# Reordering the opening of a retention-and-bilinear-FFN kernel: states and outputs in the order 0, 2, 1, 3, v scalings off VectorE, the last output in the scores' banks

## The chip, the cores and the metric

One core of one Trainium2 chip. The metric is the device time of one execution, in microseconds. Before the change it is 334.72 us (median of 4 runs, 334.57 to 334.90).

All runs named below computed the right result.

Every experiment was timed beside runs of the kernel before on the same chip in the same job. Where "over before" or "under before" is said of an experiment, it is the difference of these two medians. A ratio with an interval is the mean time of one kernel's fast runs over that of the other's of the same rounds, so it isn't quite the ratio of the medians quoted.

Names: PE is the matmul engine, PSUM the memory that it writes its results to. In the profiles DVE is VectorE, ACT is ScalarE, POOL is PoolE and SP is SyncE. The *span* of an execution runs from its first to its last instruction, and the *granted clock* is the share of PE's full clock that the profile records, so 0.5 is half clock.

## The reference, cut to what matters

```python
# q, k, v: [8 batches, 8 heads, 576 positions, 64]
scores = (1/sqrt(64)) * q @ k.T
ret    = scores * D            # D[i,j] = gamma_h ** (i-j) for i >= j, else 0
x      = (ret @ v) as [4608 tokens, 512]
out    = ((x @ w_a) * (x @ w_b)) @ w_out      # d_ff = 1536
```

The kernel splits gamma ** (i-j) into a factor on the query side (the tables `qs`, applied when an output leaves PSUM) and a factor on v (`vs`, the "v scaling"), with a triangular mask on the scores. Positions are taken in chunks, and what earlier chunks contribute is carried in a state matrix.

## The kernel before

The feed-forward part is by far the larger. It can start only when the first 512 tokens of x exist and when the first of three pieces of w_a has arrived (384 of its 1536 columns). The *opening* makes these tokens in four steps, each 256 tokens of four of the eight heads: steps 0 and 1 are the first four heads, steps 2 and 3 the others. Step 1 needs the state left by step 0; step 3 that of step 2. The order of the steps differs by kind of work: before computes scores in the order 0, 2, 1, 3, but states and outputs in the order 0, 1, 2, 3.

Each step needs loads of q, k, v (256 KB each, issued by SyncE), casts to bf16, transposes on PE with a copy out of PSUM, scores on PE with a mask on VectorE, v scaled by `vs`, a state, and an output whose scaling on VectorE writes x. `warm(n, 256)` issues n filler matmuls, meant to keep PE's clock up.

```python
    STEPS = [(0, 0), (1, 0), (0, 1), (1, 1)]
    for i, which in ((0, Q), (0, K), (2, K), (2, Q), (1, Q), (0, V),
                     (1, K), (1, V), (3, K), (3, Q), (2, V), (3, V)):
        load_step(*STEPS[i], which)                 # SyncE's queue

    def load_w(f0, f1, which="ab"):                 # weights, PoolE's queue, fp32 -> bf16
        if "a" in which:
            nc.gpsimd.dma_start(wa_sb[:, :, f0:f1], wa_r[:, :, f0:f1])
        ...
    def values_step(i, kp, on):                     # half of a step's v scaling
        n, hh = STEPS[i]
        on.tensor_tensor(...)                       # 128x256
    ...
    cast_step(2, K, "pool")                         # the opening, cut to PoolE's part
    ...
    cast_step(2, Q, "pool")
    ...
    values_step(0, 0, pool_)                        # waits for v of step 0
    values_step(0, 1, vector)
    ...
    load_w(0, W1, "a")                              # first piece of w_a
    values_step(1, 0, vector)
    ...
    state_step(3, (0,))
    for F in range(3):
        ffn_begin(F)                                # six matmuls on x of steps 0 and 1
    output_step(3)
    warm(3, 256)
```

In the traces PoolE runs its instructions in the order in which they are written. So `load_w(0, W1, "a")` is issued when PoolE is through with all PoolE work written above it (9.84 us, right behind the scaling that starts at 9.28, below). Later, two 128-row tiles (items 4 and 5) are cast with `cast(i, "dve")`: q on ScalarE, k on VectorE, v on PoolE.

## Time and profile before

| | before |
|---|---|
| median time | 334.72 us |
| span of the profiled execution | 332.6 us |
| PE busy | 324.5 us, 98% |
| seventh feed-forward matmul starts | 20.04 us |

From the profile page: part 1 (busy us and share of the span of each engine), the granted PE clock in 40 slices of the span (tenths), and the engines' shares of the chain that ended last.

```profile
PE 324.5 (98%) x3616; PEld 167.5 (50%) x3616; DVE 166.0 (50%) x305; ACT 128.2 (39%) x270; POOL 113.8 (34%) x146
...
PEclk9999999999999999999999999999999999999999
...
PE 94%; ACT 2%; DVE 2%; issue 1%; ACTq 0%; DVEq 0%
```

PE is the bound almost everywhere. The opening is different: PE does small pieces and fillers there, and what counts is the time from which the feed-forward matmuls run unbroken. I measure this by the start of the **seventh** feed-forward matmul: six can run before the last output, the seventh needs everything. From then on the program is PE-bound, so a shift of the seventh should shift the end. This is the end of the opening in the timeline of PE (start us, duration us, engine, line, operation, output and inputs, count, and in brackets the idle time before it and what ended it):

```profile
17.20 1.47 PE L754 MATMUL pa<-xT,wa_sb 128*128 128x512 bf16 x6
18.51 0.39 PE L395 MATMUL o<-qkT,state_after 128*128 128x128 bf16 x4
18.83 0.42 PE L404 MATMUL o<-sT,vb 64*64 64x128 bf16 x16
19.18 0.50 PE L836 MATMUL w<-ones 128*128 128x256 bf16 x3
20.04 0.81 PE L772 MATMUL pa<-xT,wa_sb 128*128 128x512 bf16 x3 [0.36 <-DVE xT L411]
```

L754 are the first six, L772 begins with the seventh. In between lie the last output step, three fillers, and a wait of 0.36 us for VectorE's scaling.

These are PoolE's instructions from the timeline of before between 7 and 11 us.

```profile
7.38 0.61 POOL L315 CAST qkb<-qf 128x512 bf16<-128x512 f32 x1 [0.23 <-DMA qf<-in_q_dram]
9.28 0.62 POOL L319 TENSOR_TENSOR vb<-vf,vs 128x256 bf16<-128x256 f32 x1 [1.28 <-DMA vf<-in_v_dram]
9.84 0.93 POOL L266 DMA_DIRECT2D wa_sb<-in_moe_w_a_dram  x1
```

PoolE idles 1.28 us until v of step 0 lands, scales it, and only then issues the first weight load, at 9.84 us. And these are the DMA packets of one microsecond, 12 to 13 us, by queue (packets, MB, share of the 16 engines' time, which passes 100% where packets overlap; q1 carries q, k and v, q0 the weights):

```profile
q1 hardware_dynamic: 554, 0.27, 110.9%
q0 software_dynamic: 14, 0.01, 6.9%
```

In this microsecond the weights have hardly begun (their first packet comes at 12.6 us), and q, k and v have the DMA engines almost to themselves.

### The profile page before, as it was taken

How to read it: one execution, taken by the hardware profiler on the slowest of the kernel's cores; microseconds unless marked ns; L12 is line 12 of the kernel's file. 1: busy time of each engine (PE TensorE's matmuls, PEld its weight loads, DVE VectorE, ACT ScalarE, POOL GpSimd, SP SyncE). 2: the span in 40 equal slices, each digit the busy share in tenths (PEclk: the TensorE clock that was granted, in tenths of full speed). 3: DMA queues.
4: the chain of work that ended last, by engine and by line, in shares of the span. 5: the costliest groups of instructions: out<-in, count | busy, mean ns of one | idle time of the engine just before them, and what ended most of it. 6: DMA issues, size and time to landing. Idle time of an engine off the chain costs nothing.

```text
span 332.6 us, 8646 instructions
## 1 busy us (share of the span) xinstructions
PE 324.5 (98%) x3616; PEld 167.5 (50%) x3616; DVE 166.0 (50%) x305; ACT 128.2 (39%) x270; POOL 113.8 (34%) x146
## 2 busy tenths in 40 slices
PE   6999999999999999999999999999999999999996
PEld 3744446858644554545454545454545454444443
DVE  5845446456745464566247623762476347414321
ACT  7734833434515344353134323523352334213321
POOL 4780038570548468157044503470340000000000
PEclk9999999999999999999999999999999999999999
DMA  7999999999999999897599259955960420020002
GB/s 207 254 183 208 198 224 209 233 190 183 168 207 236 220 213 257 175 220 132 131 227 213 51 140 191 203 90 142 198 105 3 131 62 0 3 95 32 2 32 95
DMA packets 146151, 50.37 MB, mean 151 GB/s; under 512 B 130624, under 2 KB 141632, under 8 KB 146112
## 3 DMA queue, kind: packets, MB, share of 16 engines
q1 hardware_dynamic: 141360, 45.10, 65.0%
q0 software_dynamic: 4752, 4.72, 8.7%
q8 instruction: 28, 0.46, 0.6%
q14 instruction: 11, 0.09, 0.1%
HBM read 37.75 MB, written 9.44 MB: 142 GB/s over the span
## 4 chain that ended last, share of the span: by engine, by line
PE 94%; ACT 2%; DVE 2%; issue 1%; ACTq 0%; DVEq 0%
PE pa L772 28%; PE pb L787 28%; PE po L807 28%; PE o L692 2%; PE o L705 1%; PE sc L666 1%; PE kv L615 1%; ACT qs L224 1%; PE kv L371 1%; PE w L836 1%; PE tp L328 0%; PE o L404 0%; PE pa L754 0%; PE sc L343 0%; ACT qkT L330 0%
## 5 line engine op out<-in xcount | busy, mean ns | idle before, releaser
L792 DVE TENSOR_TENSOR hT<-ha,pb 128x512 bf16<-128x512 bf16 (+1 forms) x120 | 75.9, 634 | 97.8 <-PE pb L787 85.4
L780 ACT CAST ha<-pa 128x512 bf16<-128x512 f32 (+1 forms) x120 | 64.8, 543 | 123.1 <-PE pa L772 122.4
L787 PE MATMUL pb<-xT,wb_sb 128*128 128x512 bf16 (+1 forms) x480 | 111.8, 358 | 0.1
L772 PE MATMUL pa<-xT,wa_sb 128*128 128x512 bf16 (+1 forms) x474 | 110.3, 358 | 1.1 <-DVE xT L532 0.6
L807 PE MATMUL po<-wo_sb,hT 128*128 128x512 bf16 (+1 forms) x444 | 97.3, 374 | 0.0
L787 PEld LDWEIGHTS <-wb_sb 128*128 128x128 bf16 x480 | 46.7, 98 | 47.3 <-issue 1.1
L772 PEld LDWEIGHTS <-wa_sb 128*128 128x128 bf16 x474 | 45.3, 98 | 46.9 <-issue 2.5
L807 PEld LDWEIGHTS <-hT 128*128 128x128 bf16 x444 | 42.4, 98 | 47.0
L555 POOL CAST qkb<-qf 64x1024 bf16<-64x1024 f32 x15 | 15.5, 1030 | 86.9 <-DMA qf<-in_q_dram 82.7
L818 DVE COPY osb<-po 128x512 f32<-128x512 f32 (+1 forms) x18 | 12.2, 676 | 44.8 <-PE po L807 44.8
L560 POOL TENSOR_TENSOR vb<-vf,vs 128x1024 bf16<-128x1024 f32 x15 | 28.5, 1902 | 8.3 <-DMA vf<-in_v_dram 4.5
L816 ACT COPY osb<-po 128x512 f32<-128x512 f32 (+1 forms) x19 | 10.9, 575 | 45.3 <-PE po L807 45.3
L714 DVE TENSOR_TENSOR xT<-o,qs 128x512 bf16<-128x512 f32 x30 | 19.6, 681 | 5.5 <-PE o L705 5.5
L634 DVE TENSOR_TENSOR sums<-kv,sums 128x256 f32<-128x256 f32 x47 | 19.9, 422 | 4.6 <-PE kv L615 3.1
L675 DVE TENSOR_TENSOR sT<-sc,mask 128x512 bf16<-128x512 f32 x30 | 19.8, 680 | 0.0
L559 POOL CAST qkb<-qf 64x512 bf16<-64x512 f32 x30 | 17.8, 619 | 1.8 <-DMA qf<-in_q_dram 1.2
L559 POOL CAST qkb<-kf 64x512 bf16<-64x512 f32 x30 | 17.6, 614 | 0.9
L646 ACT CAST states<-sums 64x512 bf16<-64x512 f32 (+1 forms) x30 | 17.2, 574 | 0.5
L555 POOL CAST qkb<-kf 64x1024 bf16<-64x1024 f32 x15 | 15.5, 1035 | 5.4 <-DMA kf<-in_k_dram 4.9
L836 PE MATMUL w<-ones 128*128 128x256 bf16 (+1 forms) x40 | 8.5, 342 | 1.5 <-DVE ones L202 1.5
L431 POOL TENSOR_TENSOR vb<-vf,vs 128x512 bf16<-128x512 f32 x2 | 2.1, 1060 | 21.7 <-DMA vf<-in_v_dram 21.7
L224 ACT ACTIVATE qs<-qs,biasq,lgp 128x384 f32<-128x384 f32 (+1 forms) x12 | 8.0, 733 | 2.4 <-DVE qs L247 2.4
(103 smaller groups left out, 158.3 us busy)
## 6 DMA issues: line engine op xcount, KB each, us to landing
qf<-in_q_dram SPq DMA_DIRECT2D x32, 256.0 KB, 4.6
kf<-in_k_dram SPq DMA_DIRECT2D x32, 256.0 KB, 5.2
vf<-in_v_dram SPq DMA_DIRECT2D x32, 256.0 KB, 5.0
out_dram<-osb SPq DMA_DIRECT2D x31, 256.0 KB, 2.2
wo_sb<-in_moe_w_out_dram POOLq DMA_DIRECT2D x3, 512.0 KB, 17.0
out_dram<-osb SPq DMA_DIRECT2D x10, 128.0 KB, 2.8
qf<-in_q_dram SPq DMA_DIRECT2D x8, 128.0 KB, 4.1
kf<-in_k_dram SPq DMA_DIRECT2D x8, 128.0 KB, 5.4
```

What stands on the lines that cost most here:

```text
L555: nc.gpsimd.tensor_copy(qkb[0:64, w], t[0:64])
L559: nc.gpsimd.tensor_copy(to[:, :, 1 - r], fro[:, :, r])
L560: nc.gpsimd.tensor_tensor(vb.rearrange("p (k h d) -> p k h d", k=2, h=H), vf.rearrange("p (k h d) -> p k h d", k=2, h=H), vs2[:, n % BL].u ...
L634: nc.vector.tensor_tensor(sums[:, i], own, prev, op=ALU.add)
L646: nc.scalar.copy(into[half(1 - r)].rearrange("p (k a) c d -> p a k (c d)", a=2)[:, 1, which.start // 2: which.stop // 2], sums[half(r)].re ...
L675: nc.vector.tensor_tensor(sT[:, on].rearrange("p c k s -> p (c k) s"), sc[:, on].rearrange("p c k s -> p (c k) s"), mask3.unsqueeze(1).to_ ...
L714: nc.vector.tensor_tensor(x_of(t0, 128).rearrange("p c (a s) -> p c a s", a=2), o[:, :, :, kp].rearrange("p a c s -> p c a s"), qs[:, :, s ...
L772: nc.tensor.matmul(pa[:, 0:n], wa_sb[:, c, fs], xT[:, c], start=(c == 0), stop=(c == NC - 1))
L780: nc.scalar.copy(ha[:, 0:n], pa[:, 0:n])
L787: nc.tensor.matmul(pb[:, 0:n], wb_sb[:, c, fs], xT[:, c], start=(c == 0), stop=(c == NC - 1))
L792: nc.vector.tensor_tensor(hT[:, F, 0:n], has[F][:, 0:n], pb[:, 0:n], op=ALU.mult)
L807: nc.tensor.matmul(po[:, 0:width], hT[:, F, u * 128:(u + 1) * 128], wo_sb[:, F, cols], start=(F == 0), stop=(F == NF - 1))
```

## The change

Its intent: get the opening's critical engines out of each other's way. The state and the output of step 2 come before those of step 1, because step 1 depends on step 0 and step 2 doesn't; the scores ran 0, 2, 1, 3 already. VectorE, busy for 13.4 of the first 20 us, keeps the work that reads PSUM and gives its v scalings after step 0 to PoolE and ScalarE. The `qs` tables are spread out instead of being made in one block. The last output goes to the PSUM banks of the scores, so it needn't wait for the scaling of the output before it.

```diff
-    for i, which in ((0, Q), (0, K), (2, K), (2, Q), (1, Q), (0, V),
-                     (1, K), (1, V), (3, K), (3, Q), (2, V), (3, V)):
+    for i, which in ((0, Q), (0, K), (0, V), (2, Q), (2, K), (1, K),
+                     (1, Q), (2, V), (3, K), (3, Q), (1, V), (3, V)):
 ... (clearing of two_states: from VectorE's start to PoolE, after the opening)
+        if on is nc.scalar:
+            for h in range(4):
+                on.mul(to[:, h], fro[:, h], by[:, h:h + 1])
 ...
-    def output_step(i):
+    def output_step(i, place=None):
 ...
+            o = place.tile([128, 2, 512], FP32, tag="sc", name="o0")
 ... (the opening's order, cut)
-    cast_step(2, K, "pool")
-    cast_step(2, Q, "pool")
-    values_step(0, 0, pool_)
-    values_step(0, 1, vector)
+    values_step(0, 0, nc.scalar)
+    values_step(0, 1, vector)
+    cast_step(2, Q, "pool")
+    cast_step(2, K, "pool")
     load_w(0, W1, "a")
 ...
+    for kp in (0, 1):
+        values_step(1, kp, pool_)
+    values_step(3, 0, nc.scalar)
+    values_step(3, 1, pool_)
+    load_w(W1, W2)
+    score_step(3)
+    state_step(1, (0,))
+    state_step(3, (0,))
+    output_step(1)
+    output_step(3, ps_sc)
     for F in range(3):
         ffn_begin(F)
-    output_step(3)
-    warm(3, 256)
```

More of the change, by code (lines that the diff above doesn't have):

```diff
@@ L191, in make_masks @@
     def make_masks():
+        nc.gpsimd.memset(two_states, 0.0)
         nc.gpsimd.iota(idxv_i, pattern=[[256, BL], [128, 2]], base=0,
@@ L202 @@
     nc.vector.memset(ones, 1.0)
+    idxp_f = const.tile([128, 6], FP32)
+    nc.vector.tensor_copy(idxp_f, idxp_i)
+    nc.vector.tensor_scalar_add(idxp_f[64:128, 4:5], idxp_f[64:128, 4:5],
+                                -float(S))
     lgp = const.tile([128, HP], FP32)
@@ L208 @@
     nc.vector.memset(biasq, math.log(scale))
-    idxp_f = const.tile([128, 6], FP32)
-    nc.vector.tensor_copy(idxp_f, idxp_i)
-    nc.vector.tensor_scalar_add(idxp_f[64:128, 4:5], idxp_f[64:128, 4:5],
-                                -float(S))
     vs = const.tile([128, H, 6], FP32)
@@ L260 @@
     state_after = const.tile([128, 2, 2, HP, 128], BF16)
-    for t in (state_after, two_states):
-        nc.vector.memset(t, 0.0)
+    nc.vector.memset(state_after, 0.0)
     def load_w(f0, f1, which="ab"):
@@ L318, in values_step @@
         n, hh = STEPS[i]
-        on.tensor_tensor(
-            by_parity(natural[n, hh][1])[:, :, kp], given(i, 2)[:, :, kp],
-            vs[:, 4 * hh:4 * hh + 4, 2 * n + kp].unsqueeze(2)
-            .to_broadcast([128, 4, D]), op=ALU.mult)
+        to, fro = by_parity(natural[n, hh][1])[:, :, kp], given(i, 2)[:, :, kp]
+        by = vs[:, 4 * hh:4 * hh + 4, 2 * n + kp]
+        if on is nc.scalar:
+            for h in range(4):
+                on.mul(to[:, h], fro[:, h], by[:, h:h + 1])
+        else:
+            on.tensor_tensor(to, fro, by.unsqueeze(2)
+                             .to_broadcast([128, 4, D]), op=ALU.mult)
     def transpose_step(i, w, on):
@@ L387, in output_step @@
         sT = scored.pop((n, hh))
-        o = ps_o[0].tile([128, 2, 512], FP32, tag="o", name="o0")
+        if place is None:
+            o = ps_o[0].tile([128, 2, 512], FP32, tag="o", name="o0")
+        else:
+            o = place.tile([128, 2, 512], FP32, tag="sc", name="o0")
         for a in (0, 1):
@@ L841 @@
     warm(8, 512)
-    for c in range(HP):
-        make_qs(c, 0, 512)
+    make_qs(0, 0, 512)
     for i in range(4):
@@ L847 @@
     cast_step(0, K, "dve")
-    transpose_step(0, Q, "dve")
-    cast_step(2, K, "pool")
-    transpose_step(0, K, "act")
+    make_qs(1, 0, 512)
+    transpose_step(0, Q, "act")
+    transpose_step(0, K, "dve")
+    values_step(0, 0, nc.scalar)
+    values_step(0, 1, vector)
+    make_qs(2, 0, 512)
+    cast_step(2, Q, "pool")
     warm(4, 256)
     score_step(0)
-    transpose_step(2, K, "act")
+    warm(3, 256)
+    state_step(0, (0, 1))
+    warm(1, 256)
+    transpose_step(2, Q, "dve")
+    cast_step(2, K, "pool")
+    cast_step(1, K, "act")
     warm(4, 256)
+    transpose_step(2, K, "dve")
+    warm(4, 256)
+    load_w(0, W1, "a")
     cast_step(1, Q, "act")
-    cast_step(2, Q, "pool")
-    transpose_step(2, Q, "act")
-    warm(4, 256)
-    transpose_step(1, Q, "dve")
-    values_step(0, 0, pool_)
-    values_step(0, 1, vector)
-    warm(2, 256)
     score_step(2)
-    cast_step(1, K, "act")
-    state_step(0, (0, 1))
-    warm(4, 256)
     transpose_step(1, K, "act")
-    load_w(0, W1, "a")
-    values_step(1, 0, vector)
-    warm(3, 256)
     output_step(0)
-    values_step(1, 1, pool_)
+    transpose_step(1, Q, "act")
+    values_step(2, 1, pool_)
+    values_step(2, 0, pool_)
+    make_qs(3, 0, 512)
     load_w(0, W1, "b")
+    warm(5, 256)
     score_step(1)
-    cast_step(3, K, "act")
-    state_step(1, (0,))
-    transpose_step(3, K, "act")
-    cast_step(3, Q, "pool")
+    warm(1, 256)
+    cast_step(3, Q, "act")
+    state_step(2, (0, 1))
+    cast_step(3, K, "pool")
     warm(4, 256)
     transpose_step(3, Q, "act")
-    values_step(2, 0, vector)
-    values_step(2, 1, pool_)
-    output_step(1)
-    state_step(2, (0, 1))
-    score_step(3)
-    values_step(3, 1, pool_)
-    warm(4, 256)
-    output_step(2)
-    values_step(3, 0, pool_)
-    load_w(W1, W2)
-    state_step(3, (0,))
+    transpose_step(3, K, "dve")
+    output_step(2)
+    for kp in (0, 1):
[6 more added lines that the diff above has]
+    state_step(3, (0,))
+    output_step(1)
+    output_step(3, ps_sc)
     for F in range(3):
         ffn_begin(F)
-    output_step(3)
-    warm(3, 256)
     load_w(W2, DFF)
```

## The prediction

> **What bounds the kernel now.** PE. The busy table gives PE 324.5 of 332.6 us; the chain of waits is 94% PE, and after 20.04 us the timeline shows only a few PE gaps (0.55 us at 55.2, 0.36 at 71.5, 0.33 at 92.6). The first 20 us differ: the PE work there is small pieces and 40 filler matmuls, and what matters is when the feed-forward matmuls can run without a break. In the timeline the first six (0.216 us apart) run from 17.2 us, then the last output step (18.51 to 19.2), three fillers and the last scaled x (VectorE, 19.30 to 19.99) come between, and the seventh starts at 20.04. I call this "FFN-7 = 20.04".
>
> **Limits inside the opening.** Twelve 256 KB loads land about 0.9 us apart, from 3.8 to 14.5 us (issue-to-landing marks). VectorE is the crowded engine: four masks of 1.22 us (start 7.70, 10.21, 13.15, 15.71), four scalings of 0.69, casts, copies, v scalings of 0.42 to 0.58. ScalarE does four qs tables in one block (3.58 to 6.63), so the second transpose copy waits until 6.54 and the scores start only at 7.16.
>
> **What the change does.**
> 1. Two qs tables (0.76 each) leave ScalarE's path to the first transposes; one VectorE memset (0.48) leaves the path to the first cast (4.85). Estimate: first scores at 6.1 to 6.3, first mask at 6.9 (it has a v scaling before it), 0.8 us earlier.
> 2. This lead is not kept: the second mask needs the loads and casts of step 2's q and k, and stays near 10.2.
> 3. VectorE loses three v scalings and its Q copies for later steps; PoolE and ScalarE take them. Four ScalarE multiplications of 128x64 replace one 128x256 operation. The Trainium skill ("ScalarE: Activation LUTs", What ACT_TABLE_LOAD costs) gives 280 ns + 0.833 N with a pointer operand, overlapping by 93: about 1.0 us for four. This trace has eight 128x18 activations in 0.98 us, 0.105 apart, so I estimate 0.6 to 1.0. Both are off VectorE.
> 4. Third and fourth masks: about 12.5 and 15.5 instead of 13.15 and 15.71.
> 5. The last two outputs no longer share the output banks, so their matmuls needn't wait for the scaling between; but the last one waits for the last mask to leave the score banks, and for the last state copies (v of steps 1 and 3 land last, 13.6 and 14.5; PoolE scales 0.62 each). The six first matmuls now come after both outputs and cover the last scaling.
>    Estimate: output 1 done at 16.6, output 3 at 17.3, x of step 1 at 17.5, FFN begins at 17.6 and runs on: FFN-7 at about 18.9 to 19.1.
>
> **Critical part.** About 1.0 us of FFN-7; filler matmuls and the order of loads cost nothing by themselves. Behind it the weights must keep up: the second pieces land 22.5 and 25.0 and are used at 24.9 and 28.3, the third at 28.1 and 31.3, used at 31.8 and about 35, w_out 33.9 to 39.4, used from 40.4. About 2.4 us of slack everywhere, so a 1 us shift fits. The rest of the program should shift as a block.
>
> **Predicted:** 333.7 us, range 333.0 to 334.5. Faster by over 2%: 0.01; within 2%: 0.98; slower by over 2%: 0.01.
>
> **What would show it.** First scores PE near 6.2; second mask near 10.2; last scaling ending before 18.5; seventh FFN matmul near 19.0, no gap before it; same PE gaps afterwards.
>
> **What would make it wrong.** The earlier weight load delaying the last v loads; ScalarE's queue, in order, holding a state copy behind a cast that waits for a load; the PoolE scalings of step 1 coming late and delaying the states; W1's second half landing after 20 us; later gaps at 55 us growing since their loads haven't moved.

## The result, and the profile after

The kernel after takes **337.21 us** (median of 4 runs, 336.79 to 337.59) against 334.72 before: ratio 1.0074, 95% interval 1.0056 to 1.0091. Measured again beside before in a later job (r_after): 337.34 against 334.77, ratio 1.0082 (1.0067 to 1.0097). It is 2.5 us slower, where about 1 us faster was predicted.

| | before | after |
|---|---|---|
| span of the profiled execution | 332.6 us | 335.1 us |
| mean granted PE clock | 1.000 | 0.995 |
| masks of the four steps start | 7.70, 10.21, 13.15, 15.71 | 6.68, 10.42, 12.63, 15.48 |
| last v landed | 14.46 us | 17.00 us |
| seventh feed-forward matmul | 20.04 us | 22.56 us |

(The landings are marks in the trace.) The span grew by 2.5 us, and so did the start of the seventh matmul. All of the loss in this profile is therefore in the opening; the PE gaps after it are those of before, shifted (0.55 us at 57.7 against 55.2, 0.36 at 74.0 against 71.5, 0.33 at 95.2 against 92.6). Up to the fourth mask the opening ran as predicted. It broke after that.

The page of after, same lines as above: there is now a slice with the clock below full, and a DMA stands in the chain that ended last.

```profile
PE 326.4 (97%) x3610; PEld 168.0 (50%) x3610; DVE 165.7 (49%) x304; ACT 129.3 (39%) x276; POOL 115.0 (34%) x147
...
PEclk9979999999999999999999999999999999999999
...
PE 91%; SPq 2%; DMA 2%; DVE 1%; ACT 1%; issue 1%; ACTq 0%; DVEq 0%
```

The end of the opening on PE:

```profile
17.42 0.94 PE L375 MATMUL kv<-vb,qkb 64*64 64x64 bf16 x8 [1.42 <-ACT vb L323]
...
20.00 0.64 PE L411 MATMUL o<-sT,vb 64*64 64x128 bf16 x16
20.57 2.15 PE L761 MATMUL pa<-xT,wa_sb 128*128 128x512 bf16 x6
22.56 0.38 PE L779 MATMUL pa<-xT,wa_sb 128*128 128x512 bf16 x1
```

PE stood for 1.42 us before a state matmul (`kv`), then ran slowly: the six feed-forward matmuls took 2.15 us instead of 1.47. The chain that ended last, in order of time (start, duration, what), says what PE stood for:

```profile
9.22 7.78 DMA vf<-in_v_dram
...
17.02 1.07 ACT vb L323 x4
...
18.13 0.22 PE kv L375 x3
18.35 0.60 PE o L402 x4
...
20.64 2.09 PE pa L761 x6
22.73 1.29 PE pa L779 x6
```

It is the last v load, 7.78 us from issue to landing. The four such loads of before take 5.3 to 5.7 us each. ScalarE's and PoolE's scalings, the state, both outputs and the feed-forward matmuls all follow behind it.

PoolE after, to be set against the three lines of before:

```profile
8.37 0.62 POOL L315 CAST qkb<-kf 128x512 bf16<-128x512 f32 x1 [0.21 <-DMA kf<-in_k_dram]
8.93 0.92 POOL L266 DMA_DIRECT2D wa_sb<-in_moe_w_a_dram  x1
...
17.07 0.62 POOL L325 TENSOR_TENSOR vb<-vf,vs 128x256 bf16<-128x256 f32 x1 [1.64 <-DMA vf<-in_v_dram]
17.63 0.81 POOL L266 DMA_DIRECT2D wa_sb<-in_moe_w_a_dram  x1
```

PoolE no longer waits for v of step 0 before the first weight load, as that v is scaled elsewhere; it still waits for q and k of step 2. The load is issued at 8.93 us, 0.91 earlier. (17.07 is the last v's scaling; behind it the second weight loads are 1.9 us later than before, but no PE wait appears for them.) The packets of the same microsecond, 12 to 13 us:

```profile
q0 software_dynamic: 180, 0.14, 88.5%
q1 hardware_dynamic: 185, 0.09, 37.4%
```

The two queues now send about as many packets each, and q, k and v get 0.09 MB in this microsecond instead of 0.27. This suggests a theory. The Trainium skill ("DMA: Bandwidth & Descriptors", Queues, rings and completion order) says that each DMA engine round-robins between the queues it has work for, "at *packet* granularity". The 180 and 185 packets agree with that. A weight packet is larger (0.14 MB in 180, against 0.09 in 185) and takes longer (88.5% of the engines' time for 180 packets, 37.4% for 185). So alternating about one for one costs q, k and v two thirds of their rate while both queues have work. Over 12 to 15 us the counts are 567 (q, k, v) and 493 (weights), so one for one is rough. How long the two share depends on when the weights begin: their first packets come at 12.6 us in before, when 0.19 of the 3.15 MB of q, k and v are still to be sent, and at 11.4 us in after, when 0.46 MB are. (The page's packet may hold several descriptors; whether the trace's packets are the same unit is not shown here.)

The last view is the table of stretches (stretch, its length, then busy us and instructions of PE, PE weight load, VectorE, ScalarE, PoolE; then the granted clock, the DMA share and GB/s):

```profile
14.00:16.00 2.00, 1.97 (x63) 1.46 (x61) 1.55 (x3) 0.65 (x2) 1.20 (x2) 1.00 1.23 206
16.00:18.00 2.00, 0.53 (x6) 0.43 (x6) 0.70 (x1) 0.98 (x5) 0.94 (x2) 1.00 0.87 137
18.00:20.00 2.00, 1.95 (x29) 1.10 (x28) 0.42 (x1) 1.01 (x5) 2.00 (x4) 0.65 0.49 31
20.00:22.00 2.00, 2.00 (x21) 0.98 (x21) 0.96 (x2) 0.00 (x0) 2.00 (x3) 0.50 1.10 171
22.00:24.00 2.00, 2.00 (x11) 0.88 (x9) 0.00 (x0) 0.81 (x2) 2.00 (x5) 1.00 1.23 203
```

After the stretch with little PE work the clock is at half for 3.4 us (18.6 to 22.0 by the trace's clock records).

### The profile page after: what moved, and what is told of

Read it like the earlier page. It is cut to its first block, busy times and chain, and to the rows that moved or that the text cites. A ratio compares the mean times of both kernels' runs of the same rounds, so it can differ in the third digit from the quotient of the medians.

```text
span 335.1 us, 8644 instructions
## 1 busy us (share of the span) xinstructions
PE 326.4 (97%) x3610; PEld 168.0 (50%) x3610; DVE 165.7 (49%) x304; ACT 129.3 (39%) x276; POOL 115.0 (34%) x147
## 2 busy tenths in 40 slices
DMA packets 146151, 50.37 MB, mean 150 GB/s; under 512 B 130624, under 2 KB 141632, under 8 KB 146112
## 4 chain that ended last, share of the span: by engine, by line
PE 91%; SPq 2%; DMA 2%; DVE 1%; ACT 1%; issue 1%; ACTq 0%; DVEq 0%
PE pb L794 28%; PE pa L779 28%; PE po L814 28%; SPq L154 2%; DMA vf<-in_v_dram 2%; PE o L699 1%; PE o L712 1%; PE sc L673 1%; PE kv L622 1%; PE pa L761 1%; PE o L402 0%; PE o L411 0%; ACT vb L323 0%; PE tp L452 0%; DVE sT L505 0%
## 5 line engine op out<-in xcount | busy, mean ns | idle before, releaser
L562 POOL CAST qkb<-qf 64x1024 bf16<-64x1024 f32 x15 | 15.5, 1031 | 84.5 <-DMA qf<-in_q_dram 69.7
L641 DVE TENSOR_TENSOR sums<-kv,sums 128x256 f32<-128x256 f32 x47 | 19.8, 422 | 4.6 <-PE kv L622 3.1
L562 POOL CAST qkb<-kf 64x1024 bf16<-64x1024 f32 x15 | 15.5, 1036 | 9.7 <-DMA kf<-in_k_dram 9.3
L843 PE MATMUL w<-ones 128*128 128x256 bf16 (+1 forms) x34 | 7.8, 357 | 1.5 <-DVE ones L203 1.5
## 6 DMA issues: line engine op xcount, KB each, us to landing
wo_sb<-in_moe_w_out_dram POOLq DMA_DIRECT2D x3, 512.0 KB, 16.6
```

The lines of the kernel that those rows point to most:

```text
L562: nc.gpsimd.tensor_copy(qkb[0:64, w], t[0:64])
L641: nc.vector.tensor_tensor(sums[:, i], own, prev, op=ALU.add)
```

## The experiments

Theory A: the earlier first weight load delays the last v loads; the stall that follows, and the clock drop that follows the stall, are the loss. Rival B: the order of steps and loads itself, or the moved fillers, causes the stall or the drop.

All outputs are right. The medians, each with before's in the same job:

| run | job | time | before | ratio (95%) | seventh matmul in its profile |
|---|---|---|---|---|---|
| e1_hold1 | 1 | 334.71 | 334.95 | 0.9995 (0.9976 to 1.0014) | 19.20 |
| e1b_hold2 | 1 | 336.18 | 334.95 | 1.0048 (1.0025 to 1.007) | 19.85 |
| e2_before_early | 1 | 337.57 | 334.95 | 1.0093 (1.0057 to 1.0129) | 25.41 |
| e3_fillers | 1 | 336.99 | 334.95 | 1.0056 (1.0037 to 1.0075) | 21.09 |
| r_before | 2 | 334.61, one run | 334.77 | - | 20.33 |
| r_after | 2 | 337.34 | 334.77 | 1.0082 (1.0067 to 1.0097) | 21.82 |
| r_hold1 (= e1) | 2 | 334.25 | 334.77 | 0.9987 (0.9971 to 1.0002) | 19.37 |
| e5_hold1_no_bank | 2 | 335.04 | 334.77 | 1.0019 (0.9985 to 1.0053) | 19.43 |
| e10_hold1_poolcasts | 3 | 333.32 | 334.58 | 0.9958 (0.9944 to 0.9972) | 18.96 |
| e11_before_poolcasts | 3 | 334.23 | 334.58 | 0.999 (0.9975 to 1.0005) | 20.80 |
| e7_after_step3_dve | 3 | 336.99 | 334.58 | 1.0063 (1.0029 to 1.0097) | 23.54 |
| e13_no_act_scales | 3 | 333.46 | 334.58 | 0.9978 (0.9953 to 1.0003) | 19.18 |
| e14_after_poolcasts | 4 | 336.61 | 334.86 | 1.0054 (1.0033 to 1.0076) | 22.30 |
| e15_fillers_poolcasts | 4 | 335.47 | 334.86 | 1.0018 (1.0 to 1.0036) | 21.34 |

### e1: hold the first weight load for about 1 us

```diff
     # in make_masks, after the opening
-        nc.gpsimd.memset(two_states, 0.0)
     # in the opening
+    nc.gpsimd.memset(two_states, 0.0)
     load_w(0, W1, "a")
```

It moves work that PoolE has to do anyhow to where it delays the issue.

> The kernel after, with PoolE's clearing of two_states (1.03 us) put just before the first weight load instead of later, so that the load is issued about 1 us later, near 9.9 us. Theory A (the first weight load, now issued 0.9 us earlier, shares the DMA engines with the last v loads and delays them): the last v lands at 14.5 to 15.2 instead of 17.0, no half-clock stretch, seventh feed-forward matmul at 18.8 to 19.5, time 333.4 to 334.3. Rival B (the new order of the loads and of the steps itself, or the fillers that were moved, cause the stall and the clock drop): the last v still lands after 16.5 or PE still stalls over 1 us, time 336 or more.

The profile agrees with theory A. The load was issued at 9.54 us, 0.61 later than in after, the clock stayed at 1.0, and PE had no wait over 0.15 us before the feed-forward part. The trace has no mark for the landing of the last v, but ScalarE begins to scale it at 14.46 us, so it was there by then. The packets of 12 to 13 us in e1 look like before's again:

```profile
q1 hardware_dynamic: 534, 0.26, 107.0%
q0 software_dynamic: 26, 0.02, 12.8%
```

and so PE, with the first and the seventh feed-forward matmul (five of the first six are in this trace, one record is missing):

```profile
17.90 1.46 PE L760 MATMUL pa<-xT,wa_sb 128*128 128x512 bf16 x5
19.20 0.59 PE L778 MATMUL pa<-xT,wa_sb 128*128 128x512 bf16 x2
```

That is 3.4 us earlier than in after. The time, 334.71 us, missed the expected 333.4 to 334.3: it is the same as before's, not clearly better. The opening was mended but its gain did not reach the end; e10 below looks for where it went.

### e1b: hold it for about 2 us

```diff
+    nc.gpsimd.memset(two_states, 0.0)
+    nc.gpsimd.memset(two_states, 0.0)
     load_w(0, W1, "a")
```

> As e1, but the clearing is done twice, so the first weight load is held by about 2 us and issued near 10.9 to 11. Theory A: the last v lands at 14.2 to 14.5, no later than in e1; but the first weights land later, 17.3 to 18, and the feed-forward start may now wait for them: seventh matmul 19.0 to 19.8, time 333.6 to 334.6. Rival B: as after, 336 or more. If e1 and e1b are alike, the overlap with the weights was the whole cause.

The last v landed at 14.62 us (expected 14.2 to 14.5), the first weights at 17.65, and the seventh matmul came at 19.85 (expected 19.0 to 19.8). The time missed: 336.18, which by itself falls into the range that the expectation gave to rival B. The trace doesn't show what B means, as v was not late, the clock was full and PE didn't stall. In the profiled execution (335.19) PE waited 0.88 us near 138 us, where scores wait for transposing DMAs; it is the fastest of six, and the others reach 337.98, one with a clock drop. What makes them slower isn't shown. Holding longer than needed gives nothing, and in the opening it costs 0.65 us against e1.

### e2: the kernel before, with only the first weight load earlier

```diff
     cast_step(2, Q, "pool")
+    load_w(0, W1, "a")
 ...
-    load_w(0, W1, "a")
```

> The kernel before, with only its first weight load moved ahead of PoolE's v scaling of step 0, so issued at about 8.0 instead of 9.84 us; step order, engines and banks as before. Theory A: the last v lands at 17 or later instead of 14.5, PE stalls and may drop to half clock, time 336.5 to 340. Rival B (order of steps or fillers): no change, 334.4 to 335.0.

The load was issued at 7.68 us. The last two v loads landed at 16.46 and 17.16 us instead of 13.65 and 14.46. From its chain:

```profile
7.97 8.50 DMA vf<-in_v_dram
...
16.61 0.80 POOL vb L319
...
21.54 0.63 PE pa L754
```

A v load took 8.50 us and the seventh matmul came at 25.41. The time is 337.57 us, 2.6 over before; the profiled execution is the worst of six (340.9, with a half-clock stretch of 6.8 us, starting at 17.3). The two executions with a clock of 0.999 or 1.0 took 336.5 us, still 1.5 over before, so here the late v costs time without the drop too. Neither the steps' order, nor the load order of q, k and v, nor an engine, nor a bank was changed here. With e1 this shows the cause in both directions: taking the earlier issue away from after mends the opening, and giving it to before breaks it. Rival B falls.

### e3: fillers where PE stood idle

```diff
     state_step(1, (0,))
+    warm(13, 256)
     state_step(3, (0,))
```

> The kernel after, with 13 more filler matmuls (about 1.4 us) between the state step of step 1 and that of step 3, where PE stood idle; loads untouched. Under theory A with the half clock as an added loss: the last v still lands near 17.0, the granted clock stays 1.0, output steps and the first six feed-forward matmuls run at full speed, seventh at 21.2 to 21.7 instead of 22.56, time 335.8 to 336.3. If the half clock is the whole loss: 334 or less. If the clock drop costs nothing: 337.

The last v landed at 16.80 us, still late. The clock stayed at full through the opening, and the seventh matmul came at 21.09, 1.5 us earlier than in after and close to the expected range. So in the profile the half clock is a loss of its own. But the time was 336.99, 2.0 over before, which missed the range and lies where the expectation had put a drop that costs nothing (337). In the profiled execution another wait of 1.55 us stands near 139.5 us, again scores waiting for transposing DMAs. All four profiles of job 1 have such a wait (0.88 to 1.55 us); none of the profiles of before and after in the first session has it. That made the split between late v and clock uncertain, so it was measured again in e14 and e15.

### r_before, r_after, r_hold1: side by side

> The kernel before, unchanged, for its trace on the chip that runs the next three. The four experiments so far show a PE gap of 0.9 to 1.6 us near 138 us (scores waiting for the transposing DMAs) that neither trace of the first session has. If it belongs to that chip and not to the changes, it should be here too when the chip is the same kind; if it comes from the changes, it should be absent here and present in the other three. Seventh feed-forward matmul at 19.9 to 20.3 us.

> The kernel after, unchanged. Last v lands near 17.0, half clock for 3.4 us, seventh feed-forward matmul near 22.5, time 2.0 to 2.8 us over before's.

> e1 again, beside after itself on one chip. Theory A: seventh feed-forward matmul at 19.3 to 19.6, 3 us earlier than after; time 0.3 to 1.0 us under before's and 2.5 to 3.4 under after's. If the first weight load isn't the cause, it lies within 0.5 us of after.

None of the four profiles of job 2 has the wait near 138 us, e1's own included. It therefore isn't a fixed property of e1. Whether before had it in job 1 wasn't profiled; why it was there stays open.

r_after repeated the loss: last v at 16.27, clock 0.995 in all six executions, 2.6 us over before. r_hold1 is 3.1 us under after, with the seventh matmul at 19.37 against 20.33 in r_before: **0.96 us earlier, the gain that the prediction had for the opening.** (These are single traces. The opening of before gives 20.04, 20.33 and, in e11, 20.80; the one held by about 1 us 19.20, 19.37 and, in e10, 18.96. The groups don't overlap, but the gain is only known as 0.7 to 1.8 us.) The time, however, is only 0.5 us under before, within the expectation but below what the opening gained, and the interval (0.9971 to 1.0002) touches 1. The profiled spans differ by 0.2 us only (332.7 against 332.9). The rest was given back on the way. In r_hold1's trace a new PE gap of 0.68 us stands at 50.37 us. VectorE and PoolE there, from the timeline:

```profile
49.00 1.03 POOL L561 CAST qkb<-qf 64x1024 bf16<-64x1024 f32 x1 [1.40 <-DMA qf<-in_q_dram]
...
49.20 1.11 DVE L434 CAST qkb<-kf 128x512 bf16<-128x512 f32 x1
...
50.37 0.34 PE L451 MATMUL tp<-identity,qkb 128*128 128x128 bf16 x3 [0.68 <-DVE qkb L434]
```

and at the same place in before:

```profile
48.92 1.03 POOL L555 CAST qkb<-qf 64x1024 bf16<-64x1024 f32 x1 [1.45 <-DMA qf<-in_q_dram]
...
49.87 0.42 DVE L428 CAST qkb<-kf 128x512 bf16<-128x512 f32 x1
```

In before, VectorE's cast of k (line 428 there, 434 here) took 0.42 us, as it started when PoolE's copy of q was nearly over. In r_hold1 PE and VectorE reach this place earlier, but PoolE's copy waits for a DMA as before and starts at about the same time. The cast now starts inside it and takes 1.11 us. It ends 0.28 us after PoolE's copy does. This agrees with the Trainium skill ("SBUF — State Buffer", Who interferes with whom): a VectorE cast in its 2-port mode and PoolE share a port pair, and whoever issues first holds it for the whole instruction. (Which mode the cast ran in, the profile doesn't say.) Other profiles agree. With 0.37 (e2), 0.54 (e1) and 1.01 us (e7) of the copy left when the cast starts, the cast ends 0.28 us after it each time. In e1b and e3 both start at the same moment; there the cast takes its 0.42 us, and the copy 1.31 and 1.30 us instead of 1.03. PE waits for the cast.

### e5: e1 without the scores' banks for the last output

```diff
-    output_step(3, ps_sc)
+    output_step(3)
```

> e1, but with the last output step in the output banks as before, not in the scores' banks. If the bank change shortens the end of the opening as predicted, the last output's matmuls wait for the scaling of step 1 (0.7 us) and the seventh feed-forward matmul moves from 19.4 to 19.9 to 20.3, time 0.5 to 0.9 us over e1. If the bank change is worth nothing, the same as e1 within 0.2 us.

The median is 0.79 us over r_hold1, as expected, but the executions lie in two heaps: 333.66, 334.04 and 334.24, and 335.83 to 337.21, two of these with a clock of 0.995. In the profiled execution PE waits 0.80 us for the scaling of step 1 before the last output, and from the start of the fourth mask to the seventh matmul it takes 4.21 us, against 3.52 in r_hold1: 0.69 longer, as predicted. The absolute 19.9 us was missed, since the loads of this execution landed about 0.5 us earlier. The banks are worth about 0.7 us in the traces; with the scatter of this run, the time alone doesn't show it.

### e10: e1 with the colliding casts on PoolE

```diff
-            cast(i, "dve")
+            cast(i, "pool")
```

> e1 (first weight load held about 1 us) plus: the q and k casts of the two 128-row tiles that follow the opening go to PoolE, which idles there, instead of ScalarE and VectorE. In e1's trace VectorE's k cast ran into a PoolE copy (1.04 us instead of 0.42 in before) and PE waited 0.4 to 0.7 us for the transposes near 50 us. If that wait is what gives back e1's earlier feed-forward start, it vanishes here, the seventh feed-forward matmul stays at 19.3 to 19.6 and the time is 0.7 to 1.2 us under before's (ratio 0.9965 to 0.998). If not, the time is as e1's, 0 to 0.6 us under before's.

**333.32 us, 1.26 under before**, a little more than expected: the only version whose interval lies wholly under 1. The gap near 50 us is down to 0.15 us (the next one is the known 0.55, now at 54.0), and the seventh matmul came at 18.96. That is earlier than e1's 19.20, but not by the casts, which start only at 40 us: it is scatter of the opening.

```profile
17.67 1.46 PE L760 MATMUL pa<-xT,wa_sb 128*128 128x512 bf16 x5
18.96 0.81 PE L778 MATMUL pa<-xT,wa_sb 128*128 128x512 bf16 x3
```

### e11: the kernel before with these casts alone

> The kernel before with these PoolE casts alone, as a control: before has no PE wait near 50 us, so the casts should be worth nothing: within 0.3 us of before. If the casts themselves are the gain, it is 0.5 us or more under before.

334.23 against 334.58: 0.35 under before, interval 0.9975 to 1.0005, so no clear effect, a little beyond the expected 0.3. The casts alone don't account for e10's gain, though a part of it, up to 0.8 us by the interval, could be theirs.

### e7: after, with ScalarE's scaling of step 3 on VectorE

```diff
-    values_step(3, 0, nc.scalar)
 ...
     score_step(3)
+    values_step(3, 0, vector)
```

> The kernel after, with ScalarE's half of the v scaling of step 3 on VectorE behind the last mask; loads untouched. Tests whether ScalarE's in-order queue (state copies of step 1 behind a scaling that waits for the last v) is a cause of its own. If it is: 1 us or more better than after, at most 1.5 us over before. If the late v alone holds the states: last v still near 16.3 to 17, gain over after at most 0.5 us, time 1.8 to 2.6 us over before, half clock still there.

336.99, 2.4 over before; the last v landed at 17.50 in the profile. So a cause of its own in ScalarE's in-order queue doesn't show. The six executions sort by their clock: 335.06 and 335.26 at 1.0, 336.94 to 337.39 at 0.995, 339.32 at 0.99. Those at 1.0 are only about 0.6 us over before.

### e13: e10 with ScalarE's v scalings on VectorE

> e10 with the v scalings that the change gave to ScalarE on VectorE instead. If taking v scalings off VectorE shortens the opening as predicted, the first and the last mask start later (0.1 to 0.4 us) and the seventh feed-forward matmul comes at 19.6 to 20.0, time 0.2 to 0.5 us over e10. If ScalarE's share is worth nothing, the same as e10 within 0.2 us.

333.46 against e10's 333.32: no difference that shows. The first mask did not start later, against the expectation (7.28, e10 7.37); the fourth did (15.94 against 15.41), and the seventh matmul came 0.22 later. ScalarE's share of the scalings is worth 0.2 us in the trace at most.

### e14 and e15: after with the casts out of the way, without and with the fillers

Both have `cast(i, "pool")`; e15 also has e3's fillers.

> The kernel after with the PoolE casts of e10, so that no collision near 50 us is in the comparison; loads and opening as after. Clock drops in most executions (mean granted clock 0.995). If the drop costs about 2 us, as e7's executions with and without it suggest (about 337.1 and 335.2), this lies 1.8 to 2.6 us over before; an execution without the drop would lie within 0.8 of before.

> The same with e3's 13 fillers: the only difference is the clock. If the clock is the larger part of the loss: clock 0.998 to 1.0 in all executions, time 0.3 to 0.9 us over before, 1.3 to 2.1 under e14. If the late v is the larger part (as e3's time in the first job, 2.0 us over before, would have it): 1.3 to 2.1 us over before, less than 0.9 under e14.

e14 is 1.75 over before (expected 1.8 to 2.6) with a clock of 0.995 or less in all six executions; e15 is 0.61 over before with 0.999 or 1.0 in all six. They differ by 1.14 us, which lies between the two readings of the expectation; e15's 0.61 over before falls into the first, in which the clock is the larger part of what after loses against before. The stretches of e14, then those of e15:

```profile
18.00:20.00 2.00, 2.00 (x41) 1.26 (x42) 0.71 (x2) 0.66 (x3) 2.00 (x4) 0.70 0.56 53
20.00:22.00 2.00, 2.00 (x6) 0.64 (x5) 0.67 (x1) 0.00 (x0) 2.00 (x4) 0.50 1.19 189
```

```profile
18.00:20.00 2.00, 1.87 (x45) 1.22 (x44) 0.70 (x2) 1.07 (x5) 2.00 (x4) 1.00 0.43 23
20.00:22.00 2.00, 1.95 (x10) 0.89 (x10) 0.67 (x1) 0.03 (x1) 2.00 (x3) 1.00 1.11 179
```

In e15 the clock column stays at 1.00 where e14's has 0.70 and 0.50. The last v was late in both (16.63 and 17.05), so e15 removes the clock's part alone. In these profiles v was 0.42 us later in e15 than in e14, so 1.14 may be too little for it.

## Why the prediction was wrong

The accounting, by differences of "over before":

| term | us | from |
|---|---|---|
| the opening as changed, with the weight load held and the casts on PoolE | -1.26 | e10 |
| the last v late | +1.87 | e15 minus e10 (0.61 + 1.26) |
| half clock after the stall | +1.14 | e14 minus e15, same job |
| casts on VectorE and ScalarE, or else unexplained | +0.82 | r_after minus e14 (2.57 - 1.75) |
| sum: the change as measured | +2.57 | r_after |

The sum is exact by construction; the terms in rows two and four compare different jobs and are good to some tenths. The fourth is not fully explained. e7's profile has the cast collision (1.29 us instead of 0.42, and a PE wait of 0.86), but neither profile of after has it, so how often it strikes after itself stays open. Both of these profiles are of the fastest execution of their job (336.79 and 336.16, where the medians are 337.21 and 337.34), so what the slower ones lose besides isn't seen in any trace. For the second row the profiles say 2.38 us (seventh matmul at 21.34 and 18.96).

Point by point:

- *First scores at 6.1 to 6.3, first mask at 6.9, second near 10.2, third 12.5, fourth 15.5*: measured 6.14, 6.68, 10.42, 12.63, 15.48. Right, within the scatter (the first mask starts between 6.7 and 7.7 in the profiles of the changed opening).
- *Four ScalarE multiplications in 0.6 to 1.0 us*: 1.07 us, 0.33 each. The formula of the Trainium skill ("ScalarE: Activation LUTs", What ACT_TABLE_LOAD costs), 280 ns + 0.833 N, gives an estimate of 333 ns for N = 64; the trace has 332. The page was right, and my extrapolation from 18-element activations was the poorer guide. Moving these scalings back to VectorE changed next to nothing (e13).
- *Seventh matmul at 18.9 to 19.1*: 22.56. Wrong as the change stands. With the weight load held it is 19.20 and 19.37 (e1), and 18.96 in e10. The count of the opening's own work was right; what it left out made the result. To hit the range to 0.1 us was partly luck, as profiles of one opening differ by some tenths.
- *"v of steps 1 and 3 land last, 13.6 and 14.5"*: **this step failed**. They landed at 14.15 and 17.00. With it fell *"output 1 done at 16.6, output 3 at 17.3"*: the outputs' last matmuls ended at 19.5 and 20.6. I took the landing times of before, 0.9 us apart up to 14.5, as given, and wrote that *"filler matmuls and the order of loads cost nothing by themselves"*. For the order of q, k and v this holds: with the same order and the weight load held, the last v landed at 14.78 (r_hold1). But the times of before were those of loads that had the DMA engines nearly to themselves, because PoolE's wait for v of step 0 kept the first weight load back until 9.84 us. The change moved that scaling off PoolE, and so moved the start of a large transfer by 0.9 us, although the diff doesn't touch that load's own line. The list of risks named it ("The earlier weight load delaying the last v loads") and put no number on it. A hint was in before's trace: its first weight packets, at 12.6 us, already meet the last 0.19 MB of q, k and v, so an earlier weight load would meet more. (The counts of 13 to 14 us there, 185 weight packets and 179 of q, k and v where 582 had gone two microseconds earlier, don't give the rate of sharing: the 179 were the last there were.)
- All sixteen profiles divide in one way. Where the first weight load was issued before the last v load, by 0.2 to 1.2 us (after, r_after, e2, e3, e7, e14, e15), the last v landed at 16.3 to 17.5. In the other nine it was issued 0.6 to 1.6 us after it, and the last v landed at 14.3 to 15.1, with no mark in e1. e7's weight load, at 9.31 us, was only 0.23 earlier than e1's. No run tells whether this order or the amount of overlap decides.
- *"so a 1 us shift fits"* for the weights: nothing in the profiles waited for them; no run contradicts it.
- *The clock* was not in the prediction at all, though fillers were. A stall of 1.4 us was followed by half clock for 3.4 us, and with the stall filled the drop stayed away (e3, e15). With the casts moved, a loss of 0.6 us over before became 1.75 by it (e15 and e14).
- *"The rest of the program should shift as a block"*: true of after. But not of e1, where VectorE came earlier and PoolE's DMA-timed copy did not, and the two collided.

## What to carry to other kernels

An engine that issues DMAs from within its compute queue, as PoolE does here, has its compute work as a timer; moving an operation off it also moved the transfer written behind it (9.84 to 8.93 us). Before trusting the landing times of a trace, ask what kept other queues quiet at that moment: here a load issued 0.9 us earlier gained 0.35 us for itself (first weights at 16.76 instead of 17.11) and cost the last v 2.5. And when a stage starts earlier, look for what stays where it was, since what was timed by PE and what was timed by DMA then meet at new places.

## What the Trainium skill lacked or had wrong

- "TensorE: Matmul & The Clock Gate" (HAM oscillation; Why this matters for your kernels) gives the rule of no PE idle gaps over about 3.4 us (about 3 in the second place). Here the clock fell to half after far shorter gaps: 1.42 us in after and 0.80 us in r_after. The gap's length alone doesn't decide: e5's profile has a PE wait of 0.80 us too, and its clock stayed full there. In the 3.41 us before the drop PE was busy for 1.90 us in after and for 2.49 us in r_after; in r_hold1, which didn't drop there, for 3.41 in the corresponding stretch. The half-clock stretches of the opening lasted 3.41 us or twice that (e2 and e7, 6.83), which agrees with the page's window. The page does tell, for another kernel, of short idles that throttle, but gives no level of activity below which a window counts as idle, and these runs don't settle one.
- "DMA: Bandwidth & Descriptors" (Queues, rings and completion order) states the round robin by packet but not its consequence when packets differ: in 12 to 13 us of after, 180 weight packets took 88.5% of the engines' time and left 185 q, k, v packets 0.09 MB, where the queue had 0.27 MB in before.
- "DMA: Bandwidth & Descriptors" (Issuing engines are not separate DMA queues) says that DMAs interleave whichever engine starts them. It doesn't add that compute on PoolE delays the DMA issues written behind it, and so can be what keeps a rival transfer back: 9.84 us against 8.93 for the first weight load, and 2.5 us for the last v.
